# The last matrix product of a fused attention and two-mixture kernel, by Strassen's scheme on halves

## The chip, the cores and the metric

The kernel runs on one core of a Trainium2 chip. Its time is the device time of one execution in microseconds (us), and the time of a version is the median of its runs. The engines are named as the profile names them: PE is TensorE (matrix products), PEld its loads of stationary weights, DVE is VectorE, ACT is ScalarE, POOL is GpSimd, SP is SyncE, which issues the DMAs. SBUF is the on-chip memory, PSUM the eight accumulator banks that PE writes (128 partitions x 512 fp32 each).

## The reference

Attention comes first (q, k, v of 4 batches, 8 heads, 576 positions, 64 channels): the sum of a banded attention (positions less than 4 apart) and an attention over means of 4 positions. Its result, 2304 tokens x 512 channels, goes through two mixtures:

```python
h = x @ w_in                                     # 512 -> 2048
x = (h * cos(h)) @ w_out                         # 2048 -> 512
xn = x / sqrt(mean(x * x) + 1e-6) * rms_g
g, val = xn @ w_gate, xn @ w_val                 # 512 -> 1536 each
out = (g / (1 + exp(-g)) * val) @ w_out2         # 1536 -> 512
```

The change is about the last line, a product of 2304 x 1536 by 1536 x 512. Every large product is done with operands split into a high part, rounded to PE's fp32r format, and the remainder as a low part: high x high + high x low + low x high, three matmuls for one.

## The kernel before

The 2304 tokens are 9 tiles of 256 (`NTILE`, `TT`), in three groups (`NG`) of three tiles (`GT`). All work is written as Python generators that ask a planner (`Order`) for engines, buffers and events: `yield "DVE", 0.7` says that the next instruction takes 0.7 us of DVE, `take` and `give` move buffers in and out of named pools, `wait` and `done` are events, `due` is a due time. The planner simulates the engines with these costs and so fixes the order of instructions on every engine and queue before anything runs; on the chip each engine works through its list in that order, held back only by semaphores. A list of alternatives, as `lo_on` returns, lets the planner choose DVE or POOL.

Attention and the first mixture fill the time up to about 500 us. Then each tile is normalised (`norm`, L1321), and `comb` (L1393) makes from it the seven activation operands of a Strassen product (Winograd's form: seven products and fifteen sums of half-sized blocks in place of eight products), each rounded into high and low parts. The three sets of operands for the three groups lie in `xc0`, `xc1` and in the space of the first mixture's activations. `splits` (L1279) does the same for each of the 12 weight columns (`C2`) of 128 inner units: four differences of 128x256 (L1298) and four rounded operands (L1312 on ACT, L1314 on DVE). Three columns are held at a time (pool `W`).

`products` (L1452) runs over 36 pairs of column and group, in the order of the list `CG`. Each pair is seven products of six matmuls 128x384 (`product`, L1433) in three PSUM banks. `ev_add` (DVE, L1515) and ACT take the sums out into SBUF buffers of a pool `tmp`, apply the gate, multiply (`ev_u`, L1549), and store the result u in DRAM (`us`). `tmp` holds 7 buffers at first, and 13 once all tiles are combined (`to_tmp`, `to_tmp2`, which takes three buffers `y` for six). A buffer is free again when its store has landed.

The output stage is ordinary. `o_loads` and `o_conv` load each of the 12 blocks of w_out2 (128x512) and round it into high and low parts; they lie in the space of `xc0` (10 blocks) and of the third set. `u_loads` and `u_conv` load u of one group and one column (128x768), and round it: one ACT and one DVE instruction. `outs` (L1626) takes for each group six banks, one for each 128 tokens, and adds up over the 12 columns: three matmuls of 512 columns each (L1650), with the tokens of u as stationary weights and w_out2 moving. `o_out` copies each bank to SBUF, by turns on ACT and DVE, and stores 128 x 512 outputs.

Of the kernel before, what the change touches and what calls it, by code (L numbers as in the profile page):

```python
# [25 lines left out]
NG = 3  # L26
GT, SW = NTILE // NG, TT // 2
C2 = DFF2 // 128
GU = 7.4
GO = 4.1  # L30
EV = 400.0
W2X = 4
NRAW = 5
# [20 lines left out]
class Order:  # L54
# [20 lines left out]
    def give(self, name, item, t=None):  # L75
        self.pools.setdefault(name, []).append((self.now() if t is None else t, item))
# [114 lines left out]
def fused_kernel(ctx: ExitStack, tc, q, k, v, w_in, w_out, w_gate, w_val, w_out2, rms_g, mask, bmask, out):  # L191
    nc = tc.nc
    PE, ACT, DVE, POOL, SP = nc.tensor, nc.scalar, nc.vector, nc.gpsimd, nc.sync
    S_ = Order()
# [27 lines left out]
    def bank_tile(i, shape, name):  # L222
        return psum.tile(shape, F32, tag=f"b{i}", name=name)
# [27 lines left out]
    def flat(src, off, ap):  # L251
        return bass.AP(src.tensor, off, ap)
# [841 lines left out]
    LAST = 8 * NTILE - 1  # L1094
    xns = dram.tile([NTILE, 128, 1024], F32, name="xns")
    wfs = dram.tile([C2, 128, 1536], F32, name="wfs")
    us = dram.tile([NG * C2, 128, 2, GT * SW], F32, name="us")
    EARLY = 3
    NP = ((0,), (1,), (2,), (3,), (4,), (5,), (6,), (7, 8))
    LATE1 = ("y", "s", "y", "s", "y", "s")  # L1100
    LATE2 = ("wf", "wf")
    CG = [(c, g) for g in range(2) for c in range(EARLY)] + [(c, 2) for c in range(EARLY)] + [(c, g) for c in range(EARLY, C2) for g in range(NG)]

    def due2(n):
        return T0 + T1 * NTILE + GU * n
# [105 lines left out]

    def to_tmp2():
        yield wait(("combs", 0))
        for x in range(3):
            x = yield take("y")
            t = x[0].tile([128, 2, 512], F32, tag=x[1], name="tmp")
            for i in range(2):
                give("tmp", t[:, i])
# [52 lines left out]
    def count2(ev, n):  # L1271
        count(ev, n)
        return cnt[ev] == n

    def lo_on(m, both):
        dve = ("DVE", 0.1 + 0.52 * m / 512, None, None, 0.3)
        return [("POOL", 0.1 + 1.35 * m / 512), dve] if both else [dve]

    def splits():  # L1279
        for c in range(C2):  # L1280
# [40 lines left out]
    def norm(t):  # L1321
# [17 lines left out]
            _, e = yield lo_on(256 * n, True)  # L1339
            (POOL if e == "POOL" else DVE).tensor_tensor(out=sq[:, 0:n], in0=sq[:, 0:n], in1=sq[:, n:2 * n], op=ALU.add)  # L1340
        sh = yield take("n1")
        yield "DVE", 0.34
        DVE.tensor_copy(out=sh[:, 0], in_=sq[:, 0])
        yield "DVE", 0.34
        DVE.tensor_tensor(out=sh[:, 1], in0=sq[:, 0], in1=sh[:, 0], op=ALU.subtract)
        p = next(p for p in NP if t in p)
        if t == p[0]:
# [13 lines left out]
        yield wait(("ms", p))  # L1361
        yield "ACT", 0.35, None, "sqrt"
        ACT.activation(out=sq[:, 0], in_=m, func=ACTF.Abs_reciprocal_sqrt, bias=cst[:, 2:3])
        yield "DVE", 0.34
# [4 lines left out]
        yield "DVE", 0.34  # L1369
        DVE.tensor_tensor(out=sq[:, 1], in0=sq[:, 1], in1=sq[:, 0], op=ALU.mult)  # L1370
        yield "DVE", 0.34
        DVE.scalar_tensor_tensor(out=sq[:, 1], in0=sq[:, 1], scalar=-3.0, in1=sq[:, 0], op0=ALU.add, op1=ALU.mult)
        for f in range(4):
            yield "DVE", 0.34
# [122 lines left out]
    def half(x):  # L1497
        return x[:, :GT * SW]
# [48 lines left out]
        yield from ev_u(n, st["u2"], st["sl"], 0)  # L1547

    def ev_u(n, v, sl, s):  # L1549
        yield "DVE", 0.47  # L1550
        DVE.tensor_tensor(out=half(v), in0=half(v), in1=half(sl), op=ALU.mult)
        give("tmp", sl)
        yield "SP", 0.6
        c, g = CG[n]
        SP.dma_start(us[g * C2 + c, :, s], half(v))
        give("tmp", v, S_.now())
        count(("us", g * C2 + c), 2)

    def o_loads():
        O = P2["O"] = {}  # L1560
        for c in range(C2):
            S_.due(due3(c) - 30.0)
            x = yield take("wo")
            S_.add(o_conv(c, x), due3(c) - 20.0)
            yield wait(("wo", c))

    def o_conv(c, t):
        done(("wo", c), 0.0)
        yield "SP", 0.8
        SP.dma_start(t, wfs[c, :, 1024:1536])  # L1570
        o = yield take("O")
        yield "ACT", 0.6
        ACT.activation(out=o[:, 0], in_=t, func=ACTF.Copy)
        yield "DVE", 0.62
        DVE.tensor_tensor(out=o[:, 1], in0=t, in1=o[:, 0], op=ALU.subtract)
        give("wo", t)
        P2["O"][c] = o
        done(("O", c))

    def u_loads():  # L1580
        for n in range(NG * C2):
            S_.due(due3(n) - 30.0)
            x = yield take("uf")
            yield wait(("us", n))
            S_.add(u_conv(n, x), due3(n) - 15.0)
            yield wait(("uf", n))

    def u_conv(n, t):
        done(("uf", n), 0.0)
        yield "SP", 1.2  # L1590
        SP.dma_start(t, us[n])
        if n:
            yield wait(("uo", n - 1))
        u = yield take("u")
        done(("uo", n), 0.0)
        yield "ACT", 0.85
        ACT.activation(out=u[:, 0], in_=t, func=ACTF.Copy)  # L1597
        yield "DVE", 0.88
        DVE.tensor_tensor(out=u[:, 1], in0=t, in1=u[:, 0], op=ALU.subtract)  # L1599
        give("uf", t)  # L1600
        P2["u", n] = u
        done(("u", n))

    def to_outs():
        yield wait(("T", C2 - 1))
        x = yield take("s")
        t = x[0].tile([128, 2, 512], F32, tag=x[1], name="wo")
        for i in range(2):
            give("wo", t[:, i])
        for n in ("s", "wf", "wf"):  # L1610
            x = yield take(n)
            give("uf", x[0].tile([128, 2, 384], F32, tag=x[1], name="uf"))
        yield wait(("gv", CG.index((C2 - 1, 0))))
        t = P2["pr"].tile([128, 10, 2, 512], F32R, tag="xc0", name="wo")
        for i in range(10):
            give("O", t[:, i])
        yield wait(("gv", CG.index((C2 - 1, 1))))
        t = P2["xcp"].tile([128, 7, 2, 2, 384], F32R, tag="xc1", name="u")
        for i in range(7):
            give("u", t[:, i])  # L1620
        yield wait(("gv", NG * C2 - 1))
        t = xr.tile([128, 2, 2, 512], F32R, tag="big", name="wo")
        for i in range(2):
            give("O", t[:, i])

    def outs():  # L1626
        S_.add(to_outs(), 0.0)
        S_.add(o_loads(), 0.0)
        S_.add(u_loads(), 0.0)
        yield wait(("gv", NG * C2 - 1))  # L1630
        S_.add(to_os(), 0.0)
        for g in range(NG):
            o, oi = {}, {}
            for c in range(C2):
                n = C2 * g + c
                yield wait(("O", c))
                yield wait(("u", n))
                u, w = P2["u", n], P2["O"][c]
                r = 0
                for s in range(2):  # L1640
                    for j in range(GT):
                        if c == 0:
                            yield take("pb")
                            i = yield take("bank")
                            oi[s, j], o[s, j] = i, bank_tile(i, [128, 512], "o")
                        S_.due(due3(n) + 0.69 * r)
                        r += 1
                        yield "PE", 0.69
                        for x, (a, b) in enumerate(((0, 0), (0, 1), (1, 0))):
                            PE.matmul(o[s, j], u[:, a, s, SW * j:SW * j + SW], w[:, b], start=(c == 0 and x == 0), stop=(c == C2 - 1 and x == 2))  # L1650
                        if c == C2 - 1:
                            S_.add(o_out(TT * (GT * g + j) + SW * s, r, o[s, j], oi[s, j]), due3(n) - 10.0)
                give("u", u)

    def to_os():
        yield wait("prods")
        for _ in range(8):
            t = yield take("tmp")
            give("os", t)

    def o_out(row, r, o, i):
        t0 = (S_.cur["t"], "PE")
        st = yield take("os")
        if r % 2:
            yield "ACT", 0.62, t0
            ACT.activation(out=st, in_=o, func=ACTF.Copy)
        else:
            yield "DVE", 0.7, t0
            DVE.tensor_copy(out=st, in_=o)
        give("bank", i)  # L1670
        give("pb", "pb")
        yield "SP", 0.96
        SP.dma_start(out[row:row + SW, :], st)
        give("os", st, S_.now())
# [58 lines left out]
```

## Time and profile before

| | us |
|---|---|
| median of 3 runs | 1019.96 (1014.98, 1019.96, 1020.24) |
| the profiled execution | 1021.67 |
| its span, first to last instruction | 1019.9 |

The profiled execution's own time is 1.8 us longer than its span. The page gives for each engine its busy time and share of the span. A stage is read from windows, which give the busy time of every engine in a stretch, and from the chain of waits, which goes back from the last instruction to what released each. A busy time of many pipelined matmuls divided by their count is the time that one adds; the mean duration of one is longer, since they overlap.

### The profile page before, as it was taken

How to read it: one execution, taken by the hardware profiler on the slowest of the kernel's cores; microseconds unless marked ns; L12 is line 12 of the kernel's file. 1: busy time of each engine (PE TensorE's matmuls, PEld its weight loads, DVE VectorE, ACT ScalarE, POOL GpSimd, SP SyncE). 2: the span in 40 equal slices, each digit the busy share in tenths (PEclk: the TensorE clock that was granted, in tenths of full speed). 3: DMA queues.
4: the chain of work that ended last, by engine and by line, in shares of the span. 5: the costliest groups of instructions: out<-in, count | busy, mean ns of one | idle time of the engine just before them, and what ended most of it. 6: DMA issues, size and time to landing. Idle time of an engine off the chain costs nothing.

```text
span 1019.9 us, 18345 instructions
## 1 busy us (share of the span) xinstructions
PE 976.4 (96%) x7048; PEld 895.8 (88%) x7048; DVE 660.1 (65%) x1180; ACT 519.4 (51%) x959; POOL 269.2 (26%) x330
## 2 busy tenths in 40 slices
PE   7888999999999999999999888999999999999998
PEld 6788899999999999888877678999999999888886
DVE  3888986457547766665689989686676656632310
ACT  3656797657748856643666765242323223421210
POOL 3947775326444411000134746000000000000000
PEclk9998999999999999999999889999999999999999
DMA  8768643344266646444643321132222312734411
GB/s 237 198 187 237 198 118 102 94 110 112 77 167 198 169 141 196 140 157 163 209 153 127 142 84 47 63 109 83 68 83 68 126 51 93 258 123 141 133 69 62
DMA packets 134056, 134.97 MB, mean 132 GB/s; under 512 B 70224, under 2 KB 108240, under 8 KB 133968
## 3 DMA queue, kind: packets, MB, share of 16 engines
q1 hardware_dynamic: 133968, 133.80, 42.8%
q8 instruction: 55, 0.90, 0.4%
q14 instruction: 33, 0.27, 0.1%
HBM read 98.12 MB, written 35.65 MB: 131 GB/s over the span
## 4 chain that ended last, share of the span: by engine, by line
PE 78%; DVE 11%; DMA 3%; POOL 2%; issue 2%; ACT 2%; SPq 2%; DVEq 0%; POOLq 0%; ACTq 0%
PE gvp L1444 24%; PE y L1053 17%; PE h L986 15%; PE o L1650 15%; PE bav L735 2%; DVE y L1375 1%; PE btr L631 1%; PE avp L579 1%; PE bs L674 1%; DMA pq<-in_q 1%; PE bat L710 1%; DVE t L1011 1%; PE sps L524 1%; DVE t L1006 1%; DMA rawwa<-in_moe_w_val 1%
## 5 line engine op out<-in xcount | busy, mean ns | idle before, releaser
L1444 PE MATMUL gvp<-xc,wc 128*128 128x384 f32 x1296 | 232.8, 336 | 3.7 <-DVE tmp L1515 3.7
L1444 PEld LDWEIGHTS gvp<-xc,wc 128*128 128x128 f32 x1296 | 225.9, 188 | 5.2 <-DVE tmp L1515 5.0
L1650 PE MATMUL o<-wo,u 128*128 128x512 f32 x648 | 148.4, 391 | 0.0
L1650 PEld LDWEIGHTS o<-wo,u 128*128 128x128 f32 x648 | 121.7, 188 | 26.5
L1515 DVE TENSOR_TENSOR tmp<-gvp,tmp 128x384 f32<-128x384 f32 x180 | 99.8, 555 | 65.8 <-PE gvp L1444 63.8
L986 PE MATMUL h<-big,wwa 128*128 128x256 f32 (+1 forms) x756 | 124.4, 317 | 0.3 <-POOL big L759 0.3
L1053 PE MATMUL y<-big,wwa 128*128 128x256 f32 (+1 forms) x672 | 114.4, 323 | 3.9 <-ACT big L1020 2.3
L986 PEld LDWEIGHTS h<-big,wwa 128*128 128x128 f32 x756 | 107.1, 191 | 9.4 <-POOL big L759 0.7
L1053 PEld LDWEIGHTS y<-big,wwa 128*128 128x128 f32 x672 | 97.4, 194 | 13.4 <-ACT big L1020 2.7
L1053 PE MATMUL y<-big,wwb 128*128 128x256 f32 (+1 forms) x504 | 83.6, 317 | 2.4 <-ACT big L1020 1.7
L986 PE MATMUL h<-big,wwb 128*128 128x256 f32 (+1 forms) x504 | 82.6, 316 | 1.1 <-DVE t L1011 1.1
L1599 DVE TENSOR_TENSOR u<-uf,u 128x768 fp32r<-128x768 f32 x36 | 34.4, 957 | 71.9 <-ACT u L1597 62.3
L1053 PEld LDWEIGHTS y<-big,wwb 128*128 128x128 f32 x504 | 71.7, 190 | 9.7 <-ACT big L1020 2.2
L986 PEld LDWEIGHTS h<-big,wwb 128*128 128x128 f32 x504 | 71.5, 190 | 7.4 <-DVE t L1011 1.5
L1597 ACT ACTIVATE u<-uf 128x768 fp32r<-128x768 f32 x36 | 30.2, 845 | 77.3 <-PE o L1650 69.3
L1006 DVE SCALAR_TENSOR_TENSOR t<-kk,h 128x512 f32<-128x512 int32 x72 | 49.0, 681 | 31.0 <-ACT kk L1004 30.6
L1004 ACT ACTIVATE kk<-h 128x512 int32<-128x512 f32 x72 | 42.5, 591 | 45.0 <-PE h L986 40.3
L1506 ACT ACTIVATE tmp<-gvp 128x384 f32<-128x384 f32 x36 | 17.7, 492 | 88.0 <-PE gvp L1444 87.9
L1009 ACT ACTIVATE t<-t,cst 128x512 f32<-128x512 f32 x72 | 51.9, 722 | 20.6 <-DVE t L1006 20.3
L1011 DVE TENSOR_TENSOR t<-h,t 128x512 f32<-128x512 f32 x72 | 49.1, 686 | 19.1 <-ACT t L1009 18.7
L1020 ACT ACTIVATE big<-t 128x512 fp32r<-128x512 f32 x72 | 45.1, 628 | 27.7 <-DVE t L1011 27.0
L759 POOL TENSOR_TENSOR big<-bt,big 128x464 fp32r<-128x464 f32 (+16 forms) x28 | 26.4, 949 | 91.4 <-ACT big L757 80.4
(174 smaller groups left out, 1576.0 us busy)
## 6 DMA issues: line engine op xcount, KB each, us to landing
us<-tmp SPq DMA_DIRECT2D x72, 192.0 KB, 1.8
uf<-us SPq DMA_DIRECT2D x36, 384.0 KB, 3.4
rawwa<-in_moe_w_out SPq DMA_DIRECT2D x21, 512.0 KB, 4.2
wfs<-rawwa SPq DMA_DIRECT2D x36, 256.0 KB, 2.5
rawwa<-in_moe_w_gate SPq DMA_DIRECT2D x12, 512.0 KB, 3.8
rawwa<-in_moe_w_val SPq DMA_DIRECT2D x12, 512.0 KB, 3.8
wf<-wfs SPq DMA_DIRECT2D x12, 512.0 KB, 3.7
vb<-in_v SPq DMA_DIRECT2D x80, 64.0 KB, 2.7
```

What stands on the lines that cost most here:

```text
L986: PE.matmul(h[:, w_ * ci:w_ * ci + w_], a[:, ksl], x_at(x, kk), start=m == 0, stop=m == 11)
L1004: ACT.activation(out=kk, in_=h, func=ACTF.Copy, scale=INV2PI, bias=0.25)
L1006: DVE.scalar_tensor_tensor(out=t, in0=kk, scalar=TWOPI, in1=h, op0=ALU.mult, op1=ALU.subtract)
L1009: ACT.activation(out=t, in_=t, func=ACTF.Sin, scale=-1.0, bias=cst[:, 0:1])
L1011: DVE.tensor_tensor(out=t, in0=h, in1=t, op=ALU.mult)
L1020: ACT.activation(out=gh, in_=t, func=ACTF.Copy)
L1053: PE.matmul(y[j][b][:, k, :], a[:, fsl], g[:, w_ * ci:w_ * ci + w_], start=(first and ci == 0 and i == 0 and k == 0), stop=(last and c == ...
L1444: PE.matmul(bank, w[:, a, kk], xc[:, x, b, kk], start=first and i == 0, stop=i == 5, skip_group_check=True)
L1515: DVE.tensor_tensor(out=half(o), in0=a, in1=half(b), op=ALU.add)
L1597: ACT.activation(out=u[:, 0], in_=t, func=ACTF.Copy)
L1599: DVE.tensor_tensor(out=u[:, 1], in0=t, in1=u[:, 0], op=ALU.subtract)
L1650: PE.matmul(o[s, j], u[:, a, s, SW * j:SW * j + SW], w[:, b], start=(c == 0 and x == 0), stop=(c == C2 - 1 and x == 2))
```

## The change

The product with w_out2 is done by the same Strassen scheme: halves of the inner rows (columns c and c + 6 make a pair, `C3` = 6 pairs), halves of the 512 output columns (256 each) and halves of the tokens of a tile (128 each). Seven banks hold the seven products of two tiles at a time (`SG`: four groups of two tiles and one of one), each bank 128 x 2 x 256, summed over the six pairs. `o_pair` makes the seven weight operands of a pair once, `u_pair` the seven activation operands of a pair for each group: four sums and four roundings (ACT for the high part, DVE for the low one). `o_ev` adds up the products as they end, one ACT copy and seven DVE additions of 128x512 a group, and stores four blocks of 256 columns for each.

Buffers move with it: the seven activation operands lie in the space of the three weight columns (`uc` from `W`, three sets), the weight operands in that of `xc0` and `xc1` (three pairs each). Two of the `y` buffers serve the output stage, so that `tmp` grows by 2 buffers in place of 6, to 9. `CG` takes the last three columns by groups: first all three for group 0, then for group 1, then for group 2. The planner's costs for some DVE and POOL instructions of the second mixture are raised (in `norm` from 0.34 to 0.36 and 0.42 us, not shown), and `us` is laid out by column and tile.

```diff
-GO = 4.1
+GO = 5.04
...
-    us = dram.tile([NG * C2, 128, 2, GT * SW], F32, name="us")
+    us = dram.tile([C2, 128, NTILE, 2, SW], F32, name="us")
     EARLY = 3
     NP = ((0,), (1,), (2,), (3,), (4,), (5,), (6,), (7, 8))
     LATE1 = ("y", "s", "y", "s", "y", "s")
     LATE2 = ("wf", "wf")
-    CG = [(c, g) for g in range(2) for c in range(EARLY)] + [(c, 2) for c in range(EARLY)] + [(c, g) for c in range(EARLY, C2) for g in range(NG)]
+    LATE = C2 - 3
+    CG = [(c, g) for g in range(NG) for c in range(EARLY)] + [(c, g) for c in range(EARLY, LATE) for g in range(NG)] \
+        + [(c, g) for g in range(NG) for c in range(LATE, C2)]
+    SG = ((0, 1), (2, 3), (4, 5), (6, 7), (8,))
+    C3 = C2 // 2
+    YB = (("y", "st"), ("y", "wo"))
...
-        for x in range(3):
+        for x in range(3 - len(YB)):
...
-        dve = ("DVE", 0.1 + 0.52 * m / 512, None, None, 0.3)
-        return [("POOL", 0.1 + 1.35 * m / 512), dve] if both else [dve]
+        dve = ("DVE", 0.15 + m / 960, None, None, 0.3)
+        return [("POOL", 0.1 + m / 330), dve] if both else [dve]
...
-        yield "DVE", 0.47
+        yield "DVE", 0.55
...
-        SP.dma_start(us[g * C2 + c, :, s], half(v))
+        SP.dma_start(us[c, :, GT * g:GT * g + GT, s], half(v).rearrange("p (j w) -> p j w", j=GT))
...
+    def o_pair(p, x):
+        done(("wo", p), 0.0)
+        f = x[0].tile([128, 2, 512], F32, tag=x[1], name="wo")
+        for k in range(2):
+            yield "SP", 0.8
+            SP.dma_start(f[:, k], wfs[p + C3 * k, :, 1024:1536])
+        w = yield take("O")
+        s = yield take("wt")
+        t = s[0].tile([128, 4, 256], F32, tag=s[1], name="wt")
+        S_.add(o_round(p, w[:, 0:2], f[:, :, 0:256], 512, x, s), S_.cur["due"])
+        S_.add(o_round(p, w[:, 6:7], f[:, 1:2, 256:512], 256, x, s), S_.cur["due"] + 1.0)
+        b11, b12, b21, b22 = (f[:, k, 256 * n:256 * n + 256] for k in range(2) for n in range(2))
+        for i, (a, b) in enumerate(((b12, b11), (b22, t[:, 0]), (b22, b12), (b21, t[:, 1]))):
+            _, e = yield lo_on(256, True)
+            (POOL if e == "POOL" else DVE).tensor_tensor(out=t[:, i], in0=a, in1=b, op=ALU.subtract)
+            if i % 2:
+                S_.add(o_round(p, w[:, i + 1:i + 3], t[:, i - 1:i + 1], 512, x, s), S_.cur["due"] + i)
+        P2["O"][p] = w
...
+    def o_round(p, w, src, m, x, s):
+        t0 = (S_.cur["t"], "POOL")
+        yield "ACT", 0.1 + 0.52 * m / 512, t0
+        ACT.activation(out=w[:, :, 0], in_=src, func=ACTF.Copy)
+        _, e = yield lo_on(m, False)
+        (POOL if e == "POOL" else DVE).tensor_tensor(out=w[:, :, 1], in0=src, in1=w[:, :, 0], op=ALU.subtract)
+        if count2(("O", p), 4):
+            give("wo", x)
+            give("wt", s)
...
+    def u_pair(n, p, ts, x):
         done(("uf", n), 0.0)
+        L = len(ts)
+        f = x[0].tile([128, 2, 2, 2, SW], F32, tag=x[1], name="uf")[:, :, :L]
+        for k in range(2):
+            yield "SP", 0.6 * L
+            SP.dma_start(f[:, k], us[p + C3 * k, :, ts[0]:ts[0] + L])
+        if n:
+            yield wait(("us1", n - 1))
+        s = yield take("st")
+        done(("us1", n), 0.0)
+        t = s[0].tile([128, 4, 2, SW], F32, tag=s[1], name="ut")[:, :, :L]
+        m = 128 * L
+        a11, a12, a21, a22 = (f[:, k, :, i] for i in range(2) for k in range(2))
+        for i, (d, a, b, op) in enumerate(((t[:, 0], a21, a22, ALU.add), (t[:, 1], t[:, 0], a11, ALU.subtract),
+                                           (t[:, 2], a11, a21, ALU.subtract), (t[:, 3], a12, t[:, 1], ALU.subtract))):
+            _, e = yield lo_on(m, False)
+            (POOL if e == "POOL" else DVE).tensor_tensor(out=d, in0=a, in1=b, op=op)
         if n:
             yield wait(("uo", n - 1))
+        u = yield take("uc")
         done(("uo", n), 0.0)
+        o = [y.rearrange("p b (c w) d -> p b c (w d)", c=2).rearrange("p b c (w d) -> p b c w d", w=2)[:, :, :, :L] for y in u[:3]]
+        o3 = u[3].rearrange("p b w d -> p b w d")[:, :, :L]
+        P2["u", n] = {0: o[0][:, :, 0], 1: o[0][:, :, 1], 2: o3, 3: o[1][:, :, 0], 4: o[1][:, :, 1], 5: o[2][:, :, 0], 6: o[2][:, :, 1]}, u
+        for i, (d, src, w) in enumerate(((o[0], f[:, :, :, 0], 2), (o[1], t[:, 0:2], 2), (o[2], t[:, 2:4], 2), (o3.unsqueeze(2), a22.unsqueeze(1), 1))):
+            S_.add(u_round(n, d, src, w * m, x, s), S_.cur["due"] + i)
...
+    def u_round(n, o, src, m, x, s):
+        t0 = (S_.cur["t"], "DVE")
+        yield "ACT", 0.1 + 0.52 * m / 512, t0
+        ACT.activation(out=o[:, 0], in_=src, func=ACTF.Copy)
+        _, e = yield lo_on(m, False)
+        (POOL if e == "POOL" else DVE).tensor_tensor(out=o[:, 1], in0=src, in1=o[:, 0], op=ALU.subtract)
+        if count2(("u", n), 4):
+            give("uf", x)
+            give("st", s)
...
     def to_outs():
         yield wait(("T", C2 - 1))
+        for a, b in (("s", "wo"), ("s", "wt"), ("wf", "uf"), ("wf", "uf"), ("s", "st")) + YB:
+            x = yield take(a)
+            give(b, x)
+        for g, (pool, tag) in enumerate(((P2["pr"], "xc0"), (P2["xcp"], "xc1"))):
+            yield wait(("gv", CG.index((C2 - 1, g))))
+            t = pool.tile([128, 3, 7, 2, 256], F32R, tag=tag, name="wo")
+            for i in range(3):
+                give("O", t[:, i])
...
+    def to_uc():
+        for i in range(3):
+            w = yield take("W")
+            if i == 0:
+                yield wait(("T", C2 - 1))
+            give("uc", w)
+        yield wait(("O", C3 - 1))
+        for n in ("wo", "wt"):
+            for _ in range(1 + sum(b == n for _, b in YB)):
+                x = yield take(n)
+                give({"wo": "uf", "wt": "st"}[n], x)
+
+
+    MO = {1: (0, 0), 6: (4, 3), 2: (1, 1), 7: (5, 4), 5: (3, 2), 4: (2, 5), 3: (6, 6)}
...
     def outs():
...
+        n = 0
+        for q, ts in enumerate(SG):
+            L = len(ts)
+            b, st = {}, {}
+            for p in range(C3):
+                yield wait(("O", p))
                 yield wait(("u", n))
+                u, w = P2["u", n], P2["O"][p]
+                for r, (m, (x, y)) in enumerate(MO.items()):
+                    if p == 0:
+                        yield take("pb")
+                        i = yield take("bank")
+                        b[m] = i, bank_tile(i, [128, 2, 256], "o")
+                    S_.due(due3(n) + 0.72 * r)
+                    yield "PE", 0.36 * L
+                    for l in range(L):
+                        for i, (j, k) in enumerate(((0, 0), (0, 1), (1, 0))):
+                            PE.matmul(b[m][1][:, l], u[0][x][:, j, l], w[:, y, k], start=(p == 0 and l == 0 and i == 0),
+                                      stop=(p == C3 - 1 and i == 2), skip_group_check=True)
+                    if p == C3 - 1:
+                        S_.add(o_ev(q, ts, m, b[m], st), due3(n) - 100.0)
+                give("uc", u[1])
+                n += 1
...
+    def o_ev(q, ts, m, b, st):
+        L = len(ts)
         t0 = (S_.cur["t"], "PE")
+        i, ps = b
+        ps = ps[:, :L]
+        need, new = {1: (None, "s1"), 6: (1, "u2"), 2: (6, "c11"), 7: (6, "u3"), 5: (7, "c22"), 4: (5, None), 3: (5, None)}[m]
+        if need:
+            yield wait(("z", q, need))
+        if new:
+            x = yield take("tmp")
+            st[new] = x, x[:, :256 * L].rearrange("p (l n) -> p l n", l=L)
+        if m == 1:
+            yield "ACT", 0.1 + 0.26 * L, t0
+            ACT.activation(out=st["s1"][1], in_=ps, func=ACTF.Copy)
         else:
+            for o, a in {6: (("u2", "s1"),), 2: (("c11", "s1"),), 7: (("u3", "u2"),), 5: (("c22", "u3"), ("u2", "u2")), 4: (("u3", "u3"),), 3: (("u2", "u2"),)}[m]:
+                yield "DVE", 0.1 + 0.3 * L, max(t0, (S_.cur["t"], "ACT"))
+                DVE.tensor_tensor(out=st[o][1], in0=ps, in1=st[a][1], op=ALU.add)
+        done(("z", q, m))
         give("bank", i)
         give("pb", "pb")
+        if m == 2:
+            give("tmp", st["s1"][0])
+        to = {2: ("c11", 0, 0), 5: ("c22", 1, 1), 4: ("u3", 1, 0), 3: ("u2", 0, 1)}.get(m)
+        if to:
+            v, s, h = to
+            yield "SP", 0.45 * L
+            SP.dma_start(flat(out, (TT * ts[0] + SW * s) * DM + 256 * h, [[DM, 128], [TT * DM, L], [1, 256]]), st[v][1])
+            give("tmp", st[v][0], S_.now())
```

## Rows read from the trace of the kernel before

**Rows 1.** The page, busy us (share of the span) x instructions.
```profile
PE 976.4 (96%) x7048; PEld 895.8 (88%) x7048; DVE 660.1 (65%) x1180; ACT 519.4 (51%) x959; POOL 269.2 (26%) x330
```

**Rows 2.** Chain of waits, last links: start, us, engine, line, count.
```profile
633.79 234.02 PE gvp L1444 x1344
867.81 148.25 PE o L1650 x648
```

**Rows 3.** Groups by form: busy us, mean ns, idle before.
```profile
L1650 PE MATMUL o<-wo,u 128*128 128x512 f32 x648 | 148.4, 391 | 0.0
L986 PE MATMUL h<-big,wwa 128*128 128x256 f32 x540 | 72.5, 287 | 0.0
```

**Rows 4.** Windows: length, busy PE, PEld, DVE, ACT, POOL, clock, DMA, GB/s.
```profile
379.50:384.50 5.00, 5.00 (x44) 5.00 (x44) 1.77 (x4) 2.03 (x4) 0.00 (x0) 1.00 0.54 167
520.00:580.00 60.00, 53.98 (x236) 43.62 (x236) 55.20 (x92) 41.89 (x65) 28.76 (x30) 0.99 0.40 141
580.00:640.00 60.00, 51.54 (x245) 46.47 (x246) 55.01 (x90) 32.45 (x60) 34.71 (x32) 0.90 0.19 68
640.00:824.00 184.00, 184.00 (x1061) 184.00 (x1061) 124.25 (x250) 55.74 (x112) 0.00 (x0) 1.00 0.26 85
900.00:960.00 60.00, 60.00 (x264) 49.26 (x263) 16.30 (x18) 14.39 (x18) 0.00 (x0) 1.00 0.37 122
```

**Rows 5.** Timeline of PE, 379 to 386 us: start, us.
```profile
379.21 5.92 PE L986 MATMUL h<-big,wwa 128*128 128x256 f32 x48
384.97 1.24 PE L986 MATMUL h<-big 128*128 128x256 f32 x9
```

**Rows 6.** Lines 1298, 1314, 1515: count, duration ns minimum/median/maximum.
```profile
L1298 DVE TENSOR_TENSOR wt<-wf,wt x21: 411/418/939, 575.9 to 808.6; 128x256 f32<-128x256 f32 x21
...
L1314 DVE TENSOR_TENSOR wc<-wt,wc x23: 677/683/1223, 568.6 to 810.9; 128x512 fp32r<-128x512 f32 x23
...
L1515 DVE TENSOR_TENSOR tmp<-gvp,tmp x180: 541/558/558, 592.9 to 869.0; 128x384 f32<-128x384 f32 x180
```

**Rows 7.** Timeline of the last column's split, 803 to 813 us.
```profile
804.46 0.62 ACT L1312 ACTIVATE wc<-wf 128x512 fp32r<-128x512 f32 x1
...
806.81 0.42 DVE L1298 TENSOR_TENSOR wt<-wf,wt 128x256 f32<-128x256 f32 x1
...
807.14 0.56 DVE L1515 TENSOR_TENSOR tmp<-gvp,tmp 128x384 f32<-128x384 f32 x1
...
809.54 0.40 ACT L1312 ACTIVATE wv<-wf 128x256 fp32r<-128x256 f32 x1
809.79 0.68 DVE L1314 TENSOR_TENSOR wc<-wt,wc 128x512 fp32r<-128x512 f32 x1
810.39 0.55 DVE L1515 TENSOR_TENSOR tmp<-gvp,tmp 128x384 f32<-128x384 f32 x1
...
811.45 0.42 DVE L1314 TENSOR_TENSOR wv<-wf,wv 128x256 fp32r<-128x256 f32 x1
```

**Rows 8.** Timeline of VectorE beside GpSimd, 593 to 596 us.
```profile
593.37 0.47 DVE L1375 SCALAR_TENSOR_TENSOR y<-y,cst,sq 128x256 f32<-128x256 f32 x1
...
594.40 1.18 POOL L1413 TENSOR_TENSOR xs<-yn 128x256 f32<-128x256 f32 x1
...
594.91 0.95 DVE L1375 SCALAR_TENSOR_TENSOR y<-y,cst,sq 128x256 f32<-128x256 f32 x1
```

**Rows 9.** DMA issues before 866 and after: count, KB each, us to landing.
```profile
us<-tmp SPq DMA_DIRECT2D x63, 192.0 KB, 1.8
...
uf<-us SPq DMA_DIRECT2D x33, 384.0 KB, 3.1
...
us<-tmp SPq DMA_DIRECT2D x2, 192.0 KB, 4.9
```

**Rows 10.** Timeline of the span's end, 1014 to 1020 us.
```profile
1015.45 0.60 ACT L1666 ACTIVATE tmp<-o 128x512 f32<-128x512 f32 x1 [0.75 <-PE o L1650]
1016.08 0.69 DVE L1669 COPY tmp<-o 128x512 f32<-128x512 f32 x1 [0.67 <-PE o L1650]
```

More of the change, by code (lines that the diff above doesn't have):

```diff
@@ L1341, in norm @@
         sh = yield take("n1")
-        yield "DVE", 0.34
+        yield "DVE", 0.36
         DVE.tensor_copy(out=sh[:, 0], in_=sq[:, 0])
-        yield "DVE", 0.34
+        yield "DVE", 0.42
         DVE.tensor_tensor(out=sh[:, 1], in0=sq[:, 0], in1=sh[:, 0], op=ALU.subtract)
@@ L1363, in norm @@
         ACT.activation(out=sq[:, 0], in_=m, func=ACTF.Abs_reciprocal_sqrt, bias=cst[:, 2:3])
-        yield "DVE", 0.34
+        yield "DVE", 0.42
         DVE.scalar_tensor_tensor(out=sq[:, 1], in0=m, scalar=1e-6, in1=sq[:, 0], op0=ALU.add, op1=ALU.mult)
@@ L1368, in norm @@
             give(tok, tok)
-        yield "DVE", 0.34
+        yield "DVE", 0.42
         DVE.tensor_tensor(out=sq[:, 1], in0=sq[:, 1], in1=sq[:, 0], op=ALU.mult)
-        yield "DVE", 0.34
+        yield "DVE", 0.42
         DVE.scalar_tensor_tensor(out=sq[:, 1], in0=sq[:, 1], scalar=-3.0, in1=sq[:, 0], op0=ALU.add, op1=ALU.mult)
         for f in range(4):
-            yield "DVE", 0.34
+            yield "DVE", 0.42
             DVE.scalar_tensor_tensor(out=y[:, f], in0=y[:, f], scalar=gv_[:, f:f + 1], in1=sq[:, 1], op0=ALU.mult, op1=ALU.mult)
@@ L1559, in o_loads @@
     def o_loads():
-        O = P2["O"] = {}
-        for c in range(C2):
-            S_.due(due3(c) - 30.0)
+        P2["O"] = {}
+        for p in range(C3):
+            S_.due(due3(p) - 50.0)
             x = yield take("wo")
[L1564 to L1578, printed above, removed]
@@ L1580, in u_loads @@
-    def u_loads():
[L1581 to L1588, printed above, removed]
-        done(("uf", n), 0.0)
-        yield "SP", 1.2
-        SP.dma_start(t, us[n])
+            S_.add(o_pair(p, x), due3(p) - 18.0)
+            yield wait(("wo", p))
+    def o_pair(p, x):
[16 more added lines that the diff above has]
+        P2["O"][p] = w
@@ new lines, in o_round @@
+    def o_round(p, w, src, m, x, s):
[7 more added lines that the diff above has]
+            give("wt", s)
+    def u_loads():
+        n = 0
+        for q, ts in enumerate(SG):
+            for p in range(C3):
+                S_.due(due3(n) - 30.0)
+                x = yield take("uf")
+                for g in sorted({t // GT for t in ts}):
+                    yield wait(("us", g * C2 + p))
+                    yield wait(("us", g * C2 + p + C3))
+                S_.add(u_pair(n, p, ts, x), due3(n) - 20.0)
+                yield wait(("uf", n))
+                n += 1
@@ L1592, in u_conv @@
         if n:
             yield wait(("uo", n - 1))
-        u = yield take("u")
+        u = yield take("uc")
         done(("uo", n), 0.0)
[L1596 to L1602, printed above, removed]
+        o = [y.rearrange("p b (c w) d -> p b c (w d)", c=2).rearrange("p b c (w d) -> p b c w d", w=2)[:, :, :, :L] for y in u[:3]]
@@ L1604, in to_outs @@
     def to_outs():
         yield wait(("T", C2 - 1))
[L1606 to L1624, printed above, removed]
+        for a, b in (("s", "wo"), ("s", "wt"), ("wf", "uf"), ("wf", "uf"), ("s", "st")) + YB:
+            x = yield take(a)
+            give(b, x)
@@ L1629, in outs @@
         S_.add(u_loads(), 0.0)
[L1630 to L1636, printed above, removed]
-                yield wait(("u", n))
[L1638 to L1661, printed above, removed]
-        t0 = (S_.cur["t"], "PE")
[L1663 to L1666, printed above, removed]
-        else:
-            yield "DVE", 0.7, t0
-            DVE.tensor_copy(out=st, in_=o)
+        yield wait(("T", C2 - 1))
+        S_.add(to_uc(), 0.0)
@@ new lines, in outs @@
+        yield wait("prods")
+        n = 0
+        for q, ts in enumerate(SG):
+            L = len(ts)
+            b, st = {}, {}
+            for p in range(C3):
+                yield wait(("O", p))
+                yield wait(("u", n))
+                u, w = P2["u", n], P2["O"][p]
[13 more added lines that the diff above has]
+                give("uc", u[1])
+                n += 1
@@ L1670, in o_out @@
         give("bank", i)
         give("pb", "pb")
-        yield "SP", 0.96
-        SP.dma_start(out[row:row + SW, :], st)
-        give("os", st, S_.now())
+        if m == 2:
[6 more added lines that the diff above has]
+            give("tmp", st[v][0], S_.now())
```

## The prediction

> **What bounds the kernel now.** I read the page first. TensorE (PE) is busy 96% of the span, VectorE (DVE) 65% [rows 1]. A mean says nothing of one stage, so the chain of waits came next: its last two links are 234.0 us of gate-and-value matmuls and then 148.25 us of output matmuls, 648 in one unbroken run [rows 2]. By form, these take 148.4 us with no idle time before them, 0.229 us each [rows 3]. The table by stage says the same: from 640 us on PE is busy for the whole of every window, clock 1.00, while DVE goes from two thirds of its time to about a quarter (16.30 of 60 us) [rows 4]. So the output stage is PE's alone, and work taken off PE there comes off the end until another engine is late. Only 520 to 640 us is different: DVE is nearly full (55.20 and 55.01 of 60 us) and PE has 14.5 us of holes, 6.0 and 8.5.
>
> **The change part by part.**
>
> *PE, output stage.* Before: 18 token blocks x 12 inner blocks x 3 matmuls (high-high, high-low, low-high) = 648 of 512 columns. After: 7 products x 6 pairs x 9 tiles x 3 = 1134 of 256 columns. The price of a 256-column matmul stands in the first mixture: 48 start at 379.21 and the next form at 384.97, 5.76/48 = 0.120 us, with PE and its weight loads (PEld) both busy throughout [rows 4, 5]. 1134 x 0.120 = 136.1 us against 148.4: **-12.3 us**. The other end is the mean of all 540 of that form, 72.5/540 = 0.134 us, which includes shorter bursts among attention work [rows 3]: 152.2 us, a loss of 3.8. I take 0.120, because the new stage is as dense as the run of 48.
>
> *DVE, output stage.* This is the cover that the change uses up. Each pair of inner blocks for two tiles now costs 4 sums of 128x256 and low parts of 3 x 128x512 and 1 x 128x256; the same set of shapes is the split of one weight column of the second mixture: 0.418 and 0.683 us [rows 6]. 5 x 0.418 + 3 x 0.683 = 4.14 us by durations. But neighbours overlap: in the last split a 0.42 us sum is followed by the next instruction after 0.33, a 0.68 us one after 0.60 [rows 7]; 0.085 less each makes 5 x 0.333 + 3 x 0.60 = 3.46 us. At the end of a group of two tiles come 7 adds of 128x512 out of PSUM, like the copy of 0.69 us [rows 10], 0.61 by starts: 4.3. A group is thus 6 x 3.46 + 4.3 = 25.1 us of DVE by starts, 6 x 4.14 + 7 x 0.69 = 29.7 by durations, against PE's 6 x 42 x 0.120 = 30.2. PE stays the bound, with 17% or 2% to spare. The last group (one tile) needs 15.1 us of PE; its 128-wide sums have no row, so I draw the line through 256 and 512 (an estimate of 0.29 us): 5 x 0.29 + 3 x 0.418 - 0.68 = 2.0 a pair, 12 in all, covered. ScalarE's share, three roundings of 0.62 and one of 0.40 per 5.04 us [rows 7], is hidden. Bytes loaded are as before.
>
> [...]
>
> *The hand-over.* Output weights need the space of the first two activation sets, free only near the end. With the last three columns ordered by token group, set 0 is free after product set 29, 234 matmuls before the end; at 234.02/1344 = 0.174 us each [rows 2] that is 40.7 us, 5.6 iterations of 42. One iteration hides one such set of DVE work beside its own sums: the last split runs from 804.46 to 811.87 inside one [rows 7], while PE stays at 184.00 of 184 us [rows 4]. So by the end of the products about 5.6 of the units are ready: four of the six weight pairs, the first activation pair and much of the second. Left before the sixth pair starts, 25.2 us later: about 6.4 units x 3.46 = 22.1 us. It fits with 3 us to spare. Against it: POOL may take the weights' differences, and a DVE instruction that meets POOL doubles (y<-y 0.47 alone, 0.95 beside POOL's sum [rows 8]); 24 such meetings are up to 11 us, so the stall is 0 to 8 us. **+2**: nearer to the rows without POOL, which is idle in the windows from 640 us on [rows 4].
>
> *Waits added.* The second product of a group waits for the bank of the previous group's first, whose ScalarE eviction, some 0.60 us [rows 10], had five products of 0.72 us to finish; the later ones have about the same lead behind DVE's adds. Behind a late product all of PE is queued, but the lead is some 3.6 us: 0. An output store on SP's queue waits for its add, and loads of the next pairs stand behind it; a load lands in 3.1 us [rows 9] and pairs are made up to three ahead: 0.
>
> *Nine temporary buffers instead of thirteen* in the products. An iteration holds eight at its peak (four of the old set, four of the new), including the store's way to DRAM, 1.8 us [rows 9]. That leaves one. Stores are now cut into runs of one tile; two stores under load took 4.9 us [rows 9], and even then old buffers return before the next set's third is taken. The split of the last column must fit between the end of column 8 and product set 29, 9 products x 1.04 = 9.4 us; it took 7.4 [rows 7]. Both together **+0.5** (0 to 4).
>
> *The planner's costs* alter no instruction, only order and the choice of DVE or POOL between 520 and 640 us, where DVE is the bound. PE's holes there are 14.5 us [rows 4]; a new order may fill or widen half of them, 7 us either way. I take **0**.
>
> *The end.* The last link is a 0.69 us copy at 1016.08 [rows 10] and a 256 KB store, 3.8 us up to the span's end. It becomes a 128x256 add and half the bytes: **-0.3** (-1 to 0).
>
> Sum: -12.3 + 2 + 0.5 + 0 - 0.3 = -10.1. The profiled execution took 1021.67 us, so 1011.6; it lies 1.7 above the median of the runs, 1019.96, hence **1010 us**.
>
> **The rivals.**
>
> *DVE costs its durations*, with no overlap left. From set 29 on, DVE needs 5.6 x 3.9 (products, 7 instructions of 0.56 [rows 6]) + 6 x 4.14 (weights) + 24 x 4.14 + 6 x 2.7 (pairs) + 4 x 4.83 (adds) = 181 us, and has 40.7 + 136.1 less the last pair's 2.5 = 174. 7 us late where I have 2: 1015 us, and a little contention makes it 1019. For: DVE is 98% full by that count. Against: the overlap in [rows 7]. Chance 0.13. [...]
>
> *Slower: activation pairs come at their latency.* One pair is load, sums, rounding, low part, and the pairs are made in order through two or three sets of buffers. A unit took 7.4 us in the products [rows 7]. With two in flight the pace is 3.7 and hidden; with 1.3 in flight, because a load waits for a buffer that waits for a rounding that waits for space, it is 5.7. Then each of 24 pairs is late by 0.66: +16, 1026 us. It decides from a pace of 5.04 us, and eats the whole gain from about 5.5. For: two load buffers until the weights are done. Against: DVE alone, without the products' sums, makes the unit in well under 7.4. Chance 0.11.
>
> *PE's weight loads set the pace.* PEld is at 5.00 of 5.00 us in the dense 256-column run [rows 4]; with other strides it might be 0.134: 1026 us. Against: 0.120 holds over 48 in a row. Chance 0.04. That is also the way in which the change would not do what it says.
>
> *The stage from 520 to 640 us shifts*: filled holes give 1003, wider ones 1017. Chance 0.12, two thirds of it for the better.
>
> **How the numbers follow.** The forecast has 0.60, with a range of its own of 1004 to 1015 us. About 0.5% is what a measurement of this kernel can tell, so faster means below 1014.9 and slower above 1025.1. Faster: 0.60 + 0.08 (better stage) + 0.04 (the lower edge of DVE's durations) = 0.72. Same: the rest of DVE's durations 0.09 and of the shifted stage 0.04, and some of the slow pairs, 0.03: 0.16. Slower: 0.12. The range reaches down to the filled holes and up past DVE's durations: 1003 to 1022.
>
> **What would show it.** Right: 1134 matmuls of 256 columns at 0.120 us, a stage of about 136 to 139 us from first to last of them; PE's few waits in the first six pairs, for a weight or activation pair from DVE; DVE 80 to 90% busy in the stage; products unbroken at 0.174. DVE's rival: DVE above 95% and PE waiting for its low parts in every group. Slow pairs: PE waiting at each pair with DVE idle, and DVE's waits ending on ScalarE or on loads. Weight loads: a cadence over 0.125 with no wait. The prediction is wrong if the output stage does not shrink by 8 us, or if the time before 640 us moves by more than the output stage does.

## The result and the profile after

The changed kernel takes 1005.1 us, the median of 6 runs (1003.69 to 1006.52), against 1020.1 (6 runs, 1014.98 to 1021.22). The ratio is 0.9859 with a 95% interval of 0.9842 to 0.9877: a gain of 12.5 to 16.1 us, more than the 10 that were forecast. It is faster, and inside the range of 1003 to 1022.

The page of the changed kernel, its engine line, answers to [rows 1]:

```profile
PE 960.6 (96%) x7534; PEld 907.3 (90%) x7534; DVE 743.5 (74%) x1425; ACT 550.4 (55%) x1052; POOL 289.5 (29%) x351
```

Its last links in the chain of waits, with the anchor used below (start, us), answer to [rows 2]:

```profile
376.11 7.20 PE h L986 x60
...
637.73 226.44 PE gvp L1449 x1302
864.17 132.68 PE o L1702 x1116
```

PE's groups by form in the output stage (busy us, mean ns, idle before), for [rows 3]:

```profile
L1702 PE MATMUL o<-wo,wc 128*128 128x256 f32 x972 | 120.6, 281 | 0.0
L1702 PE MATMUL o<-wo,wv 128*128 128x256 f32 x162 | 24.1, 281 | 0.0
```

The windows of the changed kernel, columns as in [rows 4]; the last three are the output stage:

```profile
640.00:824.00 184.00, 184.00 (x1061) 184.00 (x1060) 126.59 (x257) 56.86 (x114) 3.32 (x4) 1.00 0.30 86
864.20:900.00 35.80, 35.80 (x304) 35.80 (x303) 34.46 (x78) 16.57 (x34) 5.50 (x1) 1.00 0.51 161
900.00:960.00 60.00, 60.00 (x507) 60.00 (x506) 52.18 (x113) 26.84 (x53) 0.00 (x0) 1.00 0.47 146
960.00:998.80 38.80, 38.80 (x328) 38.79 (x326) 27.73 (x81) 14.44 (x36) 0.00 (x0) 1.00 0.23 73
```

PE has no idle time in the stage: 35.80 of 35.80, 60.00 of 60.00, 38.80 of 38.80 us. VectorE is the engine next to it, and not evenly: 34.46 of 35.80 us (96%) at first, then 52.18 of 60 (87%), then 27.73 of 38.80 (71%). The first window is the hand-over.

The two profiled executions are 17.0 us apart by their spans (1019.9 and 1002.9). To compare them stretch by stretch, both are cut at an anchor, the same 60 h matmuls, which start at 379.37 in the trace before and at 376.11 in that after. Up to the anchor they differ by 3.3 us, with the same instructions in the same order on PE, VectorE, ScalarE and GpSimd. From the anchor to the first output matmul it is 488.3 us before and 487.9 after (that matmul starts at 867.6 and at 864.0). From the first output matmul's start to the last's it is 148.0 and 134.7 us. From there to the end it is 4.2 and 4.2. So the output stage gives 13.3 us. Nothing ties the 3.3 us at the start to the change. A second trace of the unchanged kernel has the same anchor at 377.93, 1.4 us earlier than the first one:

```profile
377.93 7.20 PE h L986 x60
...
866.80 148.25 PE o L1650 x648
```

Of the kernels below, with the same list ahead of it, those with the change whose chain runs through these matmuls have the anchor between 377.5 and 378.8, those without the change between 377.9 and 378.9.

### The profile page after: what moved, and what is told of

It reads as the page before. It is cut to its first block, busy times and chain, and to the rows that moved or that the text cites. A ratio compares the mean times of both kernels' runs of the same rounds, so it can differ in the third digit from the quotient of the medians.

```text
span 1002.9 us, 19902 instructions
## 1 busy us (share of the span) xinstructions
PE 960.6 (96%) x7534; PEld 907.3 (90%) x7534; DVE 743.5 (74%) x1425; ACT 550.4 (55%) x1052; POOL 289.5 (29%) x351
## 4 chain that ended last, share of the span: by engine, by line
PE 73%; DVE 13%; DMA 3%; issue 3%; SPq 3%; ACT 2%; POOL 2%; DVEq 0%; POOLq 0%; ACTq 0%
PE gvp L1449 23%; PE y L1053 15%; PE h L986 14%; PE o L1702 13%; PE bav L735 2%; DVE y L1380 1%; DVE xc L1428 1%; PE btr L631 1%; PE avp L579 1%; DVE tmp L1520 1%; PE bs L674 1%; DVE big L1022 1%; SPq L789 1%; DVE t L1006 1%; PE sps L524 1%
## 5 line engine op out<-in xcount | busy, mean ns | idle before, releaser
L1702 PE MATMUL o<-wo,wc 128*128 128x256 f32 x972 | 120.6, 281 | 0.0
L1702 PEld LDWEIGHTS o<-wo,wc 128*128 128x128 f32 x972 | 117.8, 190 | 0.0
L1586 POOL TENSOR_TENSOR wt<-wo 128x256 f32<-128x256 f32 x10 | 9.5, 954 | 198.1 <-DVE wc L1319 172.1
L1645 ACT ACTIVATE wc<-ut 128x512 fp32r<-128x512 f32 (+1 forms) x60 | 34.4, 584 | 44.2 <-DVE ut L1631 30.6
L1022 DVE TENSOR_TENSOR big<-t,big 128x512 fp32r<-128x512 f32 x59 | 46.7, 792 | 9.7 <-ACT big L1020 9.1
```

Source lines behind the costliest of these rows:

```text
L1022: (POOL if e == "POOL" else DVE).tensor_tensor(out=gl, in0=t, in1=gh, op=ALU.subtract)
L1645: ACT.activation(out=o[:, 0], in_=src, func=ACTF.Copy)
L1702: PE.matmul(b[m][1][:, l], u[0][x][:, j, l], w[:, y, k], start=(p == 0 and l == 0 and i == 0), stop=(p == C3 - 1 and i == 2), skip_group_c ...
```

## The experiments

The theory is that the stage is PE's and costs 1134 matmuls of 256 columns at 0.118 to 0.120 us. VectorE can hide its sums behind them because its neighbouring instructions overlap: the price of one is the time from its start to the next start (0.60 us for 128x512), not its duration (0.68). The rivals are that VectorE costs its durations, that pairs come at their latency (the time of one pair from load to low part), and that the gain is from the new order or the planner's new costs.

**VectorE by itself.** PE is given a third of its work; the two products with low parts are left out:

```diff
-for i, (j, k) in enumerate(((0, 0), (0, 1), (1, 0))):
+for i, (j, k) in enumerate(((0, 0),)):
```

> The changed kernel with only the high x high matmul of each product in the output stage (the two matmuls with low parts are left out, 378 of 1134 stay); everything that VectorE and ScalarE do stays, in the same order. TensorE then needs 378 x 0.119 = 45 us for the stage, so what is left shows what feeds it. Theory (VectorE costs its starts, 25.1 us a group, 14.4 the last): the stage is VectorE's, 112 to 118 us against 134.8, the whole 984 to 990 us, VectorE over 95% busy. Rival (VectorE costs its durations, 29.7 us a group): 133 to 138 us, the whole 1003 to 1008, no gain at all. Rival (pairs come at their latency): 5 us a pair or more, 130 us or more, with VectorE idle for over 15% of the stage.

Measured 990.08 us (988.55 to 990.74), ratio 0.9699 (0.9683 to 0.9715); the output stage, from the first output matmul's start to the last's, runs from 865.8 to 981.4, 115.5 us. Its windows:

```profile
866.00:896.00 30.00, 17.47 (x94) 15.13 (x93) 28.69 (x65) 15.07 (x31) 5.47 (x1) 0.81 0.50 160
896.00:926.00 30.00, 18.46 (x93) 16.33 (x94) 30.00 (x67) 13.40 (x27) 0.00 (x0) 0.67 0.52 162
926.00:956.00 30.00, 21.44 (x119) 19.41 (x119) 29.23 (x66) 15.43 (x33) 0.00 (x0) 0.67 0.56 173
956.00:981.00 25.00, 14.97 (x73) 12.92 (x72) 24.16 (x72) 11.47 (x33) 0.00 (x0) 0.66 0.31 97
```

VectorE is busy 112.08 of 115 us, while PE waits. So the stage is VectorE's here and it needs 115.5 us. The durations' 133 to 138 are out: the 266 VectorE instructions that start in the stage have durations of 134.8 us together, more than the stage is long, so neighbours do overlap. Pairs at their latency are out too, since VectorE is not idle. Against PE's 134.7 us VectorE has 19 us to spare, 14%. PE was busy 72.34 of these 115 us and not the 45 expected, at a lower granted clock (0.66 to 0.81 in the rows); it was still not the bound.

**Loading VectorE.** One low part of each pair is made twice (`times` is 2 for one of the four), then all four are, with no change of the plan:

```diff
-        (POOL if e == "POOL" else DVE).tensor_tensor(out=o[:, 1], in0=src, in1=o[:, 0], op=ALU.subtract)
+        for _ in range(times):
+            DVE.tensor_tensor(out=o[:, 1], in0=src, in1=o[:, 0], op=ALU.subtract)
```

> The changed kernel with one of the four low parts of every activation pair made twice (one more 128x512 VectorE instruction for each of 24 pairs, one of 128x256 for the last 6); the planner is not told. Theory (starts): a group grows from 25.1 to 28.7 us, still under TensorE's 30: 1005 to 1007 us. Rival (durations): from 29.7 to 33.8, 3.8 over TensorE in four groups: 1016 to 1021 us.

> The changed kernel with all four low parts of every activation pair made twice (three more of 128x512 and one more of 128x256 a pair); the planner is not told. Theory (starts): a group needs 25.1 + 6 x 2.13 = 37.9 us of VectorE against 30, the last one 21 against 15: +34 us less a lead of a few us, 1032 to 1040 us. Rival (durations): 44.5 us a group: +60, 1060 to 1070 us.

Measured 1010.62 us (ratio 0.9901, 0.9884 to 0.9918) and 1057.61 (1.0366, 1.0349 to 1.0384): between theory and rival, and nearer to the rival for the second. Both expectations of the theory failed. The reason is in the timeline of the second kernel, where the repeat (the twin) stands right behind the instruction that it repeats. The four instructions of 2.74 us are two such couples (start, us):

```profile
945.66 0.69 DVE L1648 TENSOR_TENSOR wc<-uf,wc 128x512 fp32r<-128x512 f32 x1
946.27 2.74 DVE L1648 TENSOR_TENSOR wc<-ut,wc 128x512 fp32r<-128x512 f32 x4
948.93 0.88 DVE L1648 TENSOR_TENSOR wv<-uf,wv 128x256 fp32r<-128x256 f32 x2
...
950.06 1.41 DVE L1648 TENSOR_TENSOR wc<-uf,wc 128x512 fp32r<-128x512 f32 x2
```

A twin writes what its neighbour wrote and starts 0.72 us after it (1.41 - 0.69), not 0.60; one of 128x256 starts 0.45 after it, not 0.34. Then four twins add 3 x 0.72 + 0.45 = 2.61 us a pair, 62.6 us for 24, and about 10 for the last six, an estimate. Five of the twins, 3.3 us, are made before the stage. With the 115.5 that makes 185 us, and the stage took 184.8 (867.0 to 1051.7). The sum holds with the right price of a twin.

The changed kernel itself shows the like in one place, where a sum comes right behind the sum that it reads, at the start of a pair:

```profile
881.45 0.42 DVE L1631 TENSOR_TENSOR ut<-uf 128x256 f32<-128x256 f32 x1
881.90 0.43 DVE L1631 TENSOR_TENSOR ut<-ut,uf 128x256 f32<-128x256 f32 x1
882.25 0.69 DVE L1647 TENSOR_TENSOR wc<-uf,wc 128x512 fp32r<-128x512 f32 x1
```

It starts 0.45 us behind, just after the other's end; the low part that follows, which does not read it, 0.35 behind. So in these rows a neighbour overlaps where it does not depend on the one before it, and does not where it does. Nearly everywhere else the planner's order puts another pair's sum between two that depend on each other.

With one twin VectorE needs about 115.5 + 22 x 0.72 + 6 x 0.45 = 134.0 us, level with PE; the stage took 138.6. PE waited almost only in the first two groups, for a low part in the fifth pair and then for VectorE's additions:

```profile
886.05 1.12 PE L1703 MATMUL o<-wo,wc 128*128 128x256 f32 x8
888.62 3.62 PE L1703 MATMUL o<-wo,wc 128*128 128x256 f32 x28 [1.46 <-DVE wc L1648]
...
903.26 0.94 PE L1703 MATMUL o<-wo,wv 128*128 128x256 f32 x6 [1.00 <-DVE tmp L1727]
```

To tell the twin from the count, the repeat was put behind another low part (`again` is the pair's first low part, repeated behind the second):

```diff
-        (POOL if e == "POOL" else DVE).tensor_tensor(out=o[:, 1], in0=src, in1=o[:, 0], op=ALU.subtract)
+        DVE.tensor_tensor(out=o[:, 1], in0=src, in1=o[:, 0], op=ALU.subtract)
+        if again:
+            DVE.tensor_tensor(out=again[0][:, 1], in0=again[1], in1=again[0][:, 0], op=ALU.subtract)
```

> The changed kernel with one low part of every activation pair made twice, as in the kernel with one more low part, but the repeat stands behind another low part and not behind its twin. In the kernels with repeats a twin started 0.73 us after the instruction whose output it writes again, where unrelated neighbours start 0.60 apart. Theory (an unrelated instruction costs 0.60, a dependent one 0.73): 24 x 0.60 + 6 x 0.33 = 16.4 us on top of the 115.7 that VectorE needs by itself, 132 against TensorE's 134.7; fewer waits than with the twin beside it: 1005 to 1009 us, below the 1010.6 of that kernel. Rival (it is the added count that matters, wherever it stands): 1010 to 1012 us.

The 0.73 and 115.7 there are the 0.72 and 115.5 above. Measured 1009.16 us (0.9897, 0.9882 to 0.9912), a hair over the expectation and under the rival's, and not to be told from the twin's 0.9901 by the intervals. The totals do not decide, but the timeline does. The repeat (L1650) starts 0.60 us behind its new neighbour, and the next instruction 0.60 behind it:

```profile
934.93 0.68 DVE L1648 TENSOR_TENSOR wc<-ut,wc 128x512 fp32r<-128x512 f32 x1
935.54 0.68 DVE L1650 TENSOR_TENSOR wc<-uf,wc 128x512 fp32r<-128x512 f32 x1
936.14 0.68 DVE L1648 TENSOR_TENSOR wc<-ut,wc 128x512 fp32r<-128x512 f32 x1
```

In the single traces the stage is 137.3 us against 138.6. VectorE's mean need is now under PE's, yet PE still waits, nearly all of it in the first 33 us:

```profile
867.00:900.00 33.00, 31.58 (x264) 31.17 (x264) 31.66 (x70) 14.42 (x29) 6.09 (x1) 1.00 0.47 148
900.00:930.00 30.00, 29.80 (x249) 29.42 (x248) 30.00 (x65) 13.12 (x26) 0.00 (x0) 1.00 0.42 136
```

So the 14% is a mean over the stage; at the hand-over VectorE has next to nothing to spare.

**Width without Strassen.** The kernel before, each 512-column matmul cut in two:

```diff
-PE.matmul(o[s, j], ..., w[:, b], ...)
+for z in range(2):
+    PE.matmul(o[s, j][:, 256 * z:256 * z + 256], ..., w[:, b, 256 * z:256 * z + 256], ...)
```

> The kernel before, with each matmul of 512 columns in the output stage cut into two of 256, nothing else: 1296 in place of 648. Theory (a 256-column matmul costs 0.119 to 0.120 wherever the stage is dense): 154 to 156 us against 148.4, the whole 1025 to 1028 us; so of the 18.5 us that one product in eight would save, the narrower matmuls give back about 6. Rival (weight loads set the pace, 0.134): 174 us, 1045 us. Rival (the width costs nothing): 1020 us.

Measured 1026.07 us, ratio 1.0052 (1.0037 to 1.0067). The chain shows the stage in one run:

```profile
378.88 7.20 PE h L986 x60
...
867.19 153.13 PE o L1651 x1296
```

153.13/1296 = 0.1182 us. From the first output matmul's start to the last's it is 153.0 us against 148.0, so the width costs 5.0 us. 7/8 of 153.0 is 133.9, and the changed kernel needs 134.7. So the 13.3 us are 19.1 for one product in eight, less 5.0 for the narrower matmul and less 0.8 that is left open (0.119 us a matmul in place of 0.118). PE's weight loads don't set the pace at 0.134.

**The other edits by themselves.** The planner's costs in the kernel before, the old costs in the changed one, and the new order with nine buffers in the kernel before:

```diff
-        return [("POOL", 0.1 + 1.35 * m / 512), dve] if both else [dve]
+        return [("POOL", 0.1 + m / 330), dve] if both else [dve]
...
-        for x in range(3):
+        for x in range(1):
```

> The kernel before with the planner's new costs alone (differences and low parts, the norm's instructions, the gate's multiplication), the old output stage. Theory (the recosting only reorders 500 to 640 us and is worth nothing either way): output stage starts within 2 us of the kernel before once the two are aligned at 376 us, the whole 1017 to 1023 us. Rival (it gives part of the 15 us): 1010 to 1016 us.

> The changed kernel with the planner's old costs. Theory: the output stage keeps its 135 us, the whole 1003 to 1009 us. Rival (true costs are needed for the order in the crowded hand-over): TensorE waits at the hand-over or between groups, 1010 us or more.

> The kernel before with the new order of the last three columns and with nine temporary buffers in place of thirteen, the old output stage and the old costs. Theory: nothing in the products waits, 1018 to 1022 us. Rival (the buffers are short): waits of VectorE for stores, 3 us and more: 1023 us or more.

> The kernel before, unchanged, for a second trace. Theory (the 3 us that the trace of the changed kernel gains before 100 us, with the same instructions in the same order, differ from one execution to another): the run of 60 h matmuls near 376 to 379 us starts at another time than 379.4, by a us or more. Rival (it belongs to the program): 379.4 again.

The costs alone: 1020.82 us, ratio 0.9999 (0.9988 to 1.0010). The order and the buffers alone: 1020.32, 0.9991 (0.9975 to 1.0006). Neither shows a gain or a loss; by the interval the order could give at most 2.5 of the 15 us. The changed kernel with the old costs: 1008.67, ratio 0.9873 (0.9854 to 0.9893); its interval overlaps the changed kernel's, and its output stage is as unbroken:

```profile
377.94 7.20 PE h L986 x60
...
868.32 134.12 PE o L1702 x1128
```

In this trace the first output matmul comes 490.2 us after the anchor, where 487.9 were seen; one execution does not show that the new costs bring it forward. The second trace of the kernel before (one run, 1020.69 us) went as the theory said: its anchor is the 377.93 shown above.

**GpSimd's help.** First the activation sums may go to GpSimd (the edit below). Then the same, with PE's work cut to a third. Last, the weights' differences may not go there (`True` becomes `False` in `o_pair`):

```diff
-            _, e = yield lo_on(m, False)
+            _, e = yield lo_on(m, True)
```

> The changed kernel in which the planner may give the four sums of an activation pair to GpSimd, as it may for the weights. Theory (the stage is TensorE's, VectorE has some 19 us to spare, so help is worth nothing): 1003 to 1008 us. Rival (a VectorE instruction doubles beside GpSimd, so help costs more than it takes off): TensorE waits, 1009 us or more.

> Both: only the high x high matmul in the output stage (two of three left out), and the sums of the activation pairs may go to GpSimd. The stage was 115.7 us without GpSimd, VectorE its bound. Theory (GpSimd beside VectorE gives back nearly what it takes off): 108 to 122 us, the whole 983 to 997. Rival (GpSimd works beside VectorE for nothing, each sum moved saves 0.33 us): 85 to 105 us, the whole 960 to 980.

> The changed kernel in which the 24 differences of the output weights all go to VectorE, none to GpSimd. Theory (24 x 0.33 = 8 us more for VectorE in the stretch in which it is fullest, less what GpSimd no longer takes from it, 0.45 for each of some 21 meetings, 9 us): no change, 1003 to 1008 us. Rival (GpSimd's help carries the hand-over): TensorE waits in the first group, 1008 to 1013 us.

With GpSimd the whole took 1009.80 us, ratio 0.9901 (0.9884 to 0.9917): slower than the changed kernel, as the rival said; the theory's 1003 to 1008 failed. PE waited, chiefly for the additions at the end of groups. The timeline shows why:

```profile
895.17 0.43 DVE L1631 TENSOR_TENSOR ut<-uf 128x256 f32<-128x256 f32 x1 [1.26 <-DMA uf<-us]
...
899.16 0.97 PE L1702 MATMUL o<-wo,wc 128*128 128x256 f32 x6 [1.46 <-DVE tmp L1726]
...
907.10 1.28 DVE L1647 TENSOR_TENSOR wc<-ut,wc 128x512 fp32r<-128x512 f32 x2
...
908.04 0.94 POOL L1631 TENSOR_TENSOR ut<-uf 128x256 f32<-128x256 f32 x1 [2.96 <-DMA uf<-us]
908.30 0.96 DVE L1647 TENSOR_TENSOR wv<-uf,wv 128x256 fp32r<-128x256 f32 x1
...
909.05 0.81 POOL L1631 TENSOR_TENSOR ut<-ut,uf 128x256 f32<-128x256 f32 x1
909.18 1.22 DVE L1647 TENSOR_TENSOR wc<-uf,wc 128x512 fp32r<-128x512 f32 x1
...
909.82 1.19 POOL L1631 TENSOR_TENSOR ut<-uf 128x256 f32<-128x256 f32 x1
```

A low part of 128x256 takes 0.96 us beside GpSimd (0.41 without), one of 128x512 1.22 (0.68). Not all of the loss is this: VectorE also stood idle for late loads, 1.26 us of it shortly before PE's wait at 899. The bare stage tells the price: 78 of the 120 sums went to GpSimd, and it took 116.4 us (864.9 to 981.3, the whole 988.54 in one run) against 115.5 with none. What GpSimd takes off, it costs. The weights' differences on VectorE: 1007.34 us, ratio 0.9878 (0.9848 to 0.9909), not told from the changed kernel's; its one trace has 1.2 us of waits of PE for low parts, early in the second group. Whether GpSimd is of use there stays open.

No version tried that does the whole work beats the changed kernel.

## Why the prediction was right, and where it was off

- *PE, -12.3.* Right in kind, 1.0 us short: the stage shrank by 13.3. The price was taken as 0.120 from the first mixture [rows 5]; in this stage it is 134.7/1134 = 0.119, and 0.1182 in the old stage cut in two. The upper bound of 0.134 was never near.
- *VectorE by starts.* Confirmed: 115.5 us for the whole stage by itself, where the expectation worked out from the prediction's figures gave 112 to 118. The timeline of the changed kernel shows the starts of the sums and of the low parts that [rows 7] promised:

```profile
906.66 0.41 DVE L1631 TENSOR_TENSOR ut<-uf,ut 128x256 f32<-128x256 f32 x1
907.00 0.68 DVE L1647 TENSOR_TENSOR wc<-uf,wc 128x512 fp32r<-128x512 f32 x1
907.60 1.28 DVE L1647 TENSOR_TENSOR wc<-ut,wc 128x512 fp32r<-128x512 f32 x2
908.81 0.41 DVE L1647 TENSOR_TENSOR wv<-uf,wv 128x256 fp32r<-128x256 f32 x1
909.14 0.68 DVE L1647 TENSOR_TENSOR wc<-uf,wc 128x512 fp32r<-128x512 f32 x1
```

  0.34 us from a sum to the next instruction (duration 0.41), 0.60 from a low part to the next (0.68). In these traces this holds for independent neighbours alone: where one writes what the last one wrote it is 0.72 (128x512, in the kernel with all low parts made twice), and a sum right behind the sum that it reads starts 0.45 behind.
- *The hand-over, +2.* None was seen: PE has no wait from 864.2 us on. The meetings with GpSimd that this term stood for did come, since 21 of the 24 weights' differences ran there; they did not hold up PE. The 3 us to spare that were worked out for the sixth pair are of the right size: 0.6 to 0.7 us more a pair already make PE wait before the fourth or fifth pair, though 19 us are free over the stage.
- *Waits for banks and loads, 0.* Right for the changed kernel. They are next in line: with more work on VectorE the second thing that PE waited for was an addition at a group's end (1.00 us, in the kernel with one twin).
- *Nine buffers and column order, +0.5; costs, 0.* Both measured alone: no effect seen (0.9991 and 0.9999). Stores took 2.0 us to land in place of 1.8 [rows 9]:

```profile
us<-tmp SPq DMA_DIRECT2D x64, 192.0 KB, 2.0
```

- *The end, -0.3.* It stayed: 4.2 us from the last matmul's start, before and after. The last addition starts 1.0 us after the last matmul (999.7 and 998.7), the copy did 0.4 after (1016.1 and 1015.7). The last group's additions come one behind the other, and the 0.6 us that this adds is about what the smaller addition (0.42 us for the copy's 0.69) and store (2.8 us from there to the span's end for 3.1) give back.
- *The sum.* -10.1 was forecast and -15.0 is the difference of the medians, with an interval of 12.5 to 16.1, so the forecast fell short. The stage's 13.3 lies in it. The term that was mis-sized most is the hand-over (2 for 0), then the price of a matmul (1.0) and the buffers (0.5 for 0); the end's 0.3 did not come. What is left between 13.3 and 15.0 no stage of the traces accounts for; it is within the spread of the runs. The mechanism is the one forecast, and its signs held: VectorE is busy 85% of the stage (114.38 of 134.60 us), and the products keep 0.174 us a matmul (226.44/1302).

## What to carry to other kernels

When a stage belongs to one engine and the change pays with another one's time, take the payer's price from starts of independent neighbours (here 0.60 us for 128x512, where the duration is 0.68) and check that the order keeps dependent ones apart (the twins cost 0.72), and measure the payer by itself by cutting the bound engine's work to a third. A mean share of 85% says little: look at the busiest 30 us, where work of two stages meets. Moving sums to GpSimd was no relief here: the bare stage took 116.4 us with them there, 115.5 without.

## What the runs showed that was not expected

An instruction of VectorE that writes its predecessor's output again starts 0.72 us after it, an independent one 0.60 (128x512, duration 0.68). GpSimd's sums cost VectorE as much as they save: 116.4 us against 115.5 for the bare stage. And in the bare stage, where PE waits between pairs, its granted clock had means of 0.66 to 0.81 in the four windows, against 1.00 in the changed kernel's stage, and single matmuls of 256 columns took up to 0.58 us, where 0.29 is the longest there; this did not hurt, since VectorE was the bound.
